# One cast queue in order of need for the loads of a fused attention and MLP kernel, with the first batch's scores ahead of v

## Chip, cores and metric

One core of one Trainium2 chip. The metric is device time in microseconds (us), the median over runs of one execution each. Fast runs of one kernel mostly lie within one per cent of each other (the kernel before: 267.07 to 270.18 us over all its runs); each comparison below is with runs of the kernel before on the same chip, interleaved with it. A run is called slow when it is over 1.5% above the fastest of its kernel; slow runs are left out of ratios. In the views PE is TensorE, DVE VectorE, ACT ScalarE, POOL GpSimd and SP SyncE; the granted clock is the share of TensorE's full clock that the throttle allowed. A casting DMA turns float32 into bfloat16 on the way.

## The reference

```python
# q, k, v: (8, 8, 576, 64); phi: (8, 8, 576, 32); x has 512 columns
a = softmax(phi, over the sequence)             # 32 memory slots per head
k_m, v_m = a^T k, a^T v                         # pooled: 32 x 64 per head
attn = softmax(q k_m^T / 8) v_m                 # (8, 8, 576, 64)
x = attn with the heads side by side            # (8, 576, 512)
xn = layer norm of x, times g_ln
out = x + relu(xn @ w_ch1) @ w_ch2              # 512 -> 2048 -> 512
```

## The kernel before

The kernel works one batch at a time. For each batch: exp of phi, pooling of k and v (`a_kv`), transposes of the pooled tiles (`a_tr`), q transposed (`a_qT`), scores (`a_sc`), denominators (`a_den`), a first-layer weight folded with the pooled v (`a_w1b`; the tile is `w1b`), the exp of the scores divided by the denominators (the tile `Eh`), then the first layer (`mm1`) and, during the next batch's attention, the second (`mm2`). All 16 DMA engines load the weights W1 and W2 and the first two batches' inputs meanwhile.

```python
def load_kv(b):
    t = inp.tile([P, 4, 2, NS * D], BF16, name="kv_bf")
    if b == 2:
        # "the hold": batch 2's loads wait for the last quarter of W2
        nc.gpsimd.tensor_copy(out=t[0:1, 0, 0, 0:1], in_=w2b[0:1, 15, 0:1])
    for slot, src in ((0, k), (1, v)):
        nc.gpsimd.dma_start(out=t[:, :, slot, :], in_=rows(src, b))   # casts to bf16
    return t
...
for n in range(NCH):                       # W1, cast, on the GpSimd queue
    nc.gpsimd.dma_start(out=w1r[:, :, fs], in_=w1_v[:, :, fs])
kv1 = load_kv(1)
q1 = load_q(1)
nc.gpsimd.dma_start(out=w2b[:, 12:16, :], in_=w2_v[:, 12:16, :])
def w2_load(n, queue):                     # W2's quarters 0 to 2: float32, staged
    ...
    queue.dma_start(out=st, in_=w2_v[:, 4 * n:4 * (n + 1), :])
def w2_cast(n):                            # and cast on GpSimd
    nc.gpsimd.tensor_copy(out=w2b[:, 4 * n:4 * (n + 1), :], in_=w2_st[n])
...
def a_qT(b, i):
    if b > 0:                              # batches 1 to 7: by DMA, from SyncE's queue
        nc.sync.dma_start_transpose(out=s["qT"]..., in_=s["q"]...)
        return
    ...                                    # batch 0: on TensorE, with copies out of PSUM
```

The order in which the opening is written, which engines follow as it stands:

```python
a_kv(0); a_tr(0); a_sc(0); w1_mean(0); ... a_w1b(0, 0); a_den(0); ...     # batch 0
mm1(0, ...)
for n in range(3): w2_cast(n)
...
mm2_quarter(0); a_kv(1); a_qT(1, 0); mm2_quarter(1); ...
a_tr(1); a_w1b(1, 0); mm2(0, 0, 8, 12); a_w1b(1, 1); mm2(0, 1, 8, 12); a_sc(1); ...
mm2(0, 2, 8, 12); a_w1b(1, 2); mm2(0, 3, 8, 12); a_den(1); mm2(0, 0, 12, 16); a_w1b(1, 3)
mm2(0, 1, 12, 16); ... x_tiles(0, [4, 5]); ...
load(2, phi2)
```

The softmax here doesn't subtract the row's maximum and nothing guards it: scores larger than these inputs give would overflow.

## Time and profile before

| | before |
|---|---|
| median | 268.2 us (267.88 to 268.77, 3 runs) |
| span of the profiled run | 268.4 us (device time 270.18 us), mean granted clock 0.984 |
| first layer of batch 0 ends | 35.7 us |
| DMA transpose of batch 1's q | 44.95 to 53.46 us |
| scores of batch 1 begin | 53.6 us |
| first layer of batch 1 ends | 72.7 us |
| from there to the end | 195.7 us |

The profiled run was a long one: its device time is 2 us over the median, since a span is some 1.8 us shorter than the device time of the same run.

The last row is the steady part, in which PE is at its limit. So the row to watch is the one above it: what the opening wins or loses shows in the end of batch 1's first layer.

### The profile page before, as it was taken

How to read it: one execution, taken by the hardware profiler on the slowest of the kernel's cores; microseconds unless marked ns; L12 is line 12 of the kernel's file. 1: busy time of each engine (PE TensorE's matmuls, PEld its weight loads, DVE VectorE, ACT ScalarE, POOL GpSimd, SP SyncE). 2: the span in 40 equal slices, each digit the busy share in tenths (PEclk: the TensorE clock that was granted, in tenths of full speed). 3: DMA queues.
4: the chain of work that ended last, by engine and by line, in shares of the span. 5: the costliest groups of instructions: out<-in, count | busy, mean ns of one | idle time of the engine just before them, and what ended most of it. 6: DMA issues, size and time to landing. Idle time of an engine off the chain costs nothing.

```text
span 268.4 us, 5722 instructions
## 1 busy us (share of the span) xinstructions
PE 249.3 (93%) x2437; PEld 137.2 (51%) x2437; DVE 153.3 (57%) x302; ACT 128.0 (48%) x218; POOL 30.2 (11%) x47
## 2 busy tenths in 40 slices
PE   6887897698999999999999999999999999999992
PEld 4653554134754476447643575447543664466440
DVE  2227652439447853777385943795386646783431
ACT  3166661055725456347636284448435472555210
POOL 8310022820030001200120003000000000000000
PEclk9999999689999999999999999999999999999998
DMA  6999999999999356984798194956621471120233
GB/s 195 227 206 219 295 283 295 157 199 218 258 160 223 82 144 125 161 183 85 181 169 175 41 238 70 221 123 150 80 65 44 86 190 42 43 61 17 46 74 78
DMA packets 45058, 39.63 MB, mean 148 GB/s; under 512 B 19940, under 2 KB 38376, under 8 KB 45032
## 3 DMA queue, kind: packets, MB, share of 16 engines
q0 software_dynamic: 14784, 16.19, 36.7%
q1 hardware_dynamic: 29720, 22.49, 35.0%
q10 hardware_dynamic: 528, 0.59, 0.7%
q8 instruction: 19, 0.31, 0.4%
q14 instruction: 7, 0.06, 0.1%
HBM read 41.42 MB, written 9.44 MB: 189 GB/s over the span
## 4 chain that ended last, share of the span: by engine, by line
PE 71%; DMA 19%; ACT 4%; DVE 3%; issue 1%; DVEq 0%; POOLq 0%
PE ch_ps L397 40%; PE h_ps L339 21%; DMA q_bf<-in_q_dram 12%; DMA kv_bf<-in_k_dram 4%; DMA qT<-q_bf 3%; PE o_ps L367 3%; PE w1b_ps L318 2%; PE kv_ps L208 2%; DVE Eh L303 2%; ACT rden L300 1%; PE sc_ps L281 1%; ACT x_sb L371 1%; DVE bst L375 1%; PE den_ps L298 1%; PE kv_ps L215 1%
## 5 line engine op out<-in xcount | busy, mean ns | idle before, releaser
L397 PE MATMUL ch_ps<-w2b,rT 128*128 128x512 bf16 x576 | 136.4, 384 | 3.0 <-POOL w2b L148 3.0
L397 PEld LDWEIGHTS <-rT 128*128 128x128 bf16 x576 | 54.4, 98 | 66.4 <-issue 11.8
L339 PE MATMUL h_ps<-Eh,w1b 128*128 128x288 bf16 x512 | 66.9, 285 | 3.5 <-ACT rT L345 1.7
L345 ACT ACTIVATE rT<-h_ps 128x576 bf16<-128x576 f32 x88 | 52.5, 649 | 31.2 <-PE h_ps L339 31.0
L339 PEld LDWEIGHTS <-w1b 128*128 128x128 bf16 x512 | 49.5, 97 | 20.8 <-issue 5.1
L322 DVE SCALAR_TENSOR_TENSOR w1b<-m_sb,rsum,w1b_ps 128x512 bf16<-128x512 f32 x64 | 43.6, 738 | 8.3 <-PE w1b_ps L318 6.2
L347 DVE TENSOR_SCALAR rT<-h_ps 128x576 bf16<-128x576 f32 x40 | 30.2, 756 | 27.3 <-PE h_ps L339 27.3
L405 DVE SCALAR_TENSOR_TENSOR x_sb<-ch_ps,rstd,x_sb 128x512 f32<-128x512 f32 x36 | 26.6, 742 | 16.1 <-PE ch_ps L397 16.1
L371 ACT ACTIVATE x_sb<-o_ps 128x1024 f32<-128x1024 f32 (+1 forms) x20 | 18.7, 939 | 35.3 <-PE o_ps L367 35.3
L375 DVE BATCH_NORM_STATS2 bst<-x_sb 128x6 f32<-128x512 f32 x36 | 24.4, 677 | 8.3 <-ACT x_sb L371 8.3
L286 ACT ACTIVATE E_sb<-sc_ps,rs 128x640 bf16<-128x640 f32 x16 | 11.8, 791 | 20.2 <-PE sc_ps L281 20.2
L303 DVE SCALAR_TENSOR_TENSOR Eh<-E_sb,rs,rden 128x576 bf16<-128x576 bf16 x16 | 12.4, 814 | 14.7 <-ACT rden L302 14.7
L83 POOL DMA_DIRECT2D kv_bf<-in_k_dram x8 | 6.2, 770 | 101.3 <-PE kv_ps L215 100.2
L383 ACT ACTIVATE rstd<-mv,eps_sb 128x2 f32<-128x2 f32 (+1 forms) x20 | 5.9, 294 | 16.3 <-DVE mv L376 16.3
L187 PE MATMUL w_ps<-vmask,blk 128*128 128x256 bf16 x72 | 11.1, 319 | 2.4 <-DVE vmask L130 2.4
L367 PE MATMUL o_ps<-vb,Eh 128*128 128x256 bf16 (+1 forms) x80 | 12.0, 276 | 1.0 <-DVE Eh L303 1.0
L318 PE MATMUL w1b_ps<-w1r,kvT 64*32 64x512 bf16 x256 | 11.6, 390 | 1.1 <-DVE kvT L239 0.6
L300 ACT ACTIVATE rden<-den_ps 128x576 f32<-128x576 f32 x16 | 9.6, 644 | 4.2 <-PE den_ps L298 4.1
L226 DVE CAST v<-kv_ps 128x128 bf16<-128x128 f32 x8 | 2.3, 290 | 15.7 <-ACT k L224 15.7
L196 ACT ACTIVATE e_sb<-phi_st 128x1152 bf16<-128x1152 f32 x8 | 9.2, 1151 | 2.7 <-DMA phi_st<-in_phi_dram 2.7
L187 PEld LDWEIGHTS <-blk 128*128 128x128 bf16 x72 | 7.9, 113 | 4.3 <-DVE blk L126 1.5
L302 ACT ACTIVATE rden<-rden 128x576 f32<-128x576 f32 x16 | 10.0, 682 | 0.0
(58 smaller groups left out, 115.4 us busy)
## 6 DMA issues: line engine op xcount, KB each, us to landing
out_dram<-x_sb SPq DMA_DIRECT2D x72, 128.0 KB, 2.4
kv_bf<-in_k_dram POOLq DMA_DIRECT2D x8, 576.0 KB, 6.4
kv_bf<-in_v_dram POOLq DMA_DIRECT2D x8, 576.0 KB, 9.7
phi_st<-in_phi_dram SPq DMA_DIRECT2D x7, 576.0 KB, 4.6
q_bf<-in_q_dram POOLq DMA_DIRECT2D x7, 576.0 KB, 11.1
w_st<-in_moe_w_ch_dram SPq DMA_DIRECT2D x3, 1024.0 KB, 16.2
w1r<-in_moe_w_ch_dram POOLq DMA_DIRECT2D x4, 512.0 KB, 17.2
q_st<-in_q_dram SPq DMA_DIRECT2D x1, 1152.0 KB, 10.8
```

The source lines that it names most:

```text
L187: nc.tensor.matmul(w_ps[:, 0:256], blk, vmask.rearrange("p j d -> p (j d)"), start=True, stop=True)
L303: nc.vector.scalar_tensor_tensor(out=Eh[:, g, :], in0=s["E"][:, g, 0:S], scalar=s["rs"][:, g:g + 1], in1=rd[:, g].rearrange("p a x -> p (a ...
L318: nc.tensor.matmul(ps[32 * j:32 * (j + 1), g, :], s["kvT"][r:r + 64, 2, 32 * j:32 * (j + 1)], w1r[r:r + 64, j, fs], start=True, stop=True, ...
L322: nc.vector.scalar_tensor_tensor(out=s["w1b"][:, g, fs], in0=m_sb[:, fs], scalar=s["rsum"][:, g:g + 1], in1=ps[:, g, :], op0=ALU.mult, op1 ...
L339: nc.tensor.matmul(h_ps[:, half, 0:HS], s["w1b"][:, g, P * j:P * (j + 1)], s["Eh"][:, g, HS * half:HS * (half + 1)], start=(g == 0), stop= ...
L345: nc.scalar.activation(out=dst, in_=h_ps[:, :, 0:HS], func=AF.Relu)
L347: nc.vector.tensor_scalar(out=dst, in0=h_ps[:, :, 0:HS], scalar1=0.0, scalar2=None, op0=ALU.max)
L367: nc.tensor.matmul(ov[:, :, g, :], s["Eh"][:, g, a:z], s["vb"][:, g].rearrange("p j d -> p (j d)"), start=True, stop=True)
L371: nc.scalar.activation(out=x[:, 0:n], in_=o_ps[:, 0:n], func=AF.Copy)
L375: nc.vector.bn_stats(out=stt, in_=x[:, i, :])
L397: nc.tensor.matmul(ch_ps, rT[:, j, P * t:P * (t + 1)], w2b[:, j, :], start=(j == 0), stop=(j == JC - 1))
L405: nc.vector.scalar_tensor_tensor(out=x, in0=ch_ps, scalar=rstd, in1=x, op0=ALU.mult, op1=ALU.add)
```

## The change

The intent: drop the float32 staging of W2 and its casts on GpSimd; put everything except phi of most batches on one casting queue, in the order in which it is needed (batch 1's phi, q, k and v between W2's quarters); load q of batch 0 first; and in batch 0 pool and score k before v arrives. With it the order of batch 1's attention among the second-layer groups changes.

```diff
 def load_kv(b):
-    if b == 2:
-        nc.gpsimd.tensor_copy(out=t[0:1, 0, 0, 0:1], in_=w2b[0:1, 15, 0:1])
...
-kv1 = load_kv(1)
-q1 = load_q(1)
-nc.gpsimd.dma_start(out=w2b[:, 12:16, :], in_=w2_v[:, 12:16, :])
-w2_load(0, nc.sync)          # staged, cast later on GpSimd by w2_cast
-w2_load(1, nc.sync)
-w2_load(2, nc.sync)
+w2_load(0)                   # now a casting DMA on the GpSimd queue
+phi1 = load_phi(1, nc.gpsimd)
+q1 = load_q(1)
+w2_load(1)
+kv1 = load_kv(1)
+w2_load(2)
+w2_load(3)
...
-a_kv(0)
-a_tr(0)
-a_sc(0)
+a_k(0)
+a_tr(0, v_part=False)
+a_sc(0)
+a_v(0)
+a_den(0)
+a_tr(0, k_part=False)
...
-for n in range(3):
-    w2_cast(n)
 a_exp(1)
+a_qT(1, 0)                   # the DMA transpose is now issued before the second layer
...
 mm2_quarter(0)
-a_kv(1)
-a_qT(1, 0)
 mm2_quarter(1)
+a_kv(1)
...                           # w1b(1, 1..3) later, between the last second-layer groups;
                              # x tiles 4 and 5 moved from here into batch 1's loop
```

Cut: `phi_st` gets two buffers instead of one, the warm-up matmuls at the start become fewer, and half of the copies of batch 0's transposed q go to DVE.

## The prediction

> **What bounds the kernel now.** I read the page first, then the chain that ended last, then clock and timeline of the first 75 us. From 67 us on the kernel is a stream of matmuls; what can change lies before.
>
> ```profile
> PE   6887897698999999999999999999999999999992
> PEclk9999999689999999999999999999999999999998
> DMA  6999999999999356984798194956621471120233
> ```
>
> Each digit is 6.7 us. PE is full except in the first eight slices, and DMA is full in just these. The only clock loss, the 6 and the 8, lies at 47 to 60 us. The chain says what the start waits for:
>
> ```profile
> 1.23 11.54 DMA kv_bf<-in_k_dram
> ...
> 13.06 31.87 DMA q_bf<-in_q_dram
> ...
> 44.95 8.51 DMA qT<-q_bf
> ...
> 53.60 0.74 PE sc_ps L281 x13
> 54.33 1.40 PE ch_ps L397 x4
> ```
>
> Columns: start, length. Batch 1's q stood in the queue behind W1 and k and v until 44.95, and its transpose behind that, so batch 1's scores began only at 53.60. The second thing on the path is W2:
>
> ```profile
> 47.01 1.89 POOL L148 CAST w2b<-w_st 128x2048 bf16<-128x2048 f32 x1 [4.80 <-DMA w_st<-in_moe_w_ch_dram]
> 48.95 1.86 PE L397 MATMUL ch_ps<-w2b,rT 128*128 128x512 bf16 x4 [1.92 <-POOL w2b L148]
> ```
>
> A staged part landed at 47.0, its cast on POOL took 1.89 us, and PE stood for it. The clock, by microsecond (the column after POOL's count is PEclk):
>
> ```profile
> 47.00:48.00 1.00, 0.03 (x8) 0.06 (x1) 0.89 (x2) 0.00 (x0) 0.99 (x1) 1.00 2.29 175
> 48.00:49.00 1.00, 0.04 (x1) 0.04 (x1) 0.51 (x1) 0.00 (x0) 0.90 (x1) 0.67 0.76 90
> 49.00:50.00 1.00, 1.00 (x3) 0.35 (x3) 0.00 (x0) 0.00 (x0) 0.18 (x1) 0.50 0.28 42
> ...
> 55.00:56.00 1.00, 1.00 (x11) 0.25 (x10) 0.00 (x0) 0.61 (x1) 0.19 (x1) 0.92 1.19 200
> ```
>
> The stall put PE at half clock from 48.34 (0.67 in that microsecond) to 55.16: 6.8 us, some 3 us lost. After that the end of the stage belongs to DVE:
>
> ```profile
> 59.32 1.55 DVE L303 SCALAR_TENSOR_TENSOR Eh<-E_sb,rs,rden 128x576 bf16<-128x576 bf16 x2 [1.77 <-ACT rden L302]
> 60.78 0.75 DVE L405 SCALAR_TENSOR_TENSOR x_sb<-ch_ps,rstd,x_sb 128x512 f32<-128x512 f32 x1
> 61.44 1.40 DVE L322 SCALAR_TENSOR_TENSOR w1b<-m_sb,rsum,w1b_ps 128x512 bf16<-128x512 f32 x2
> ...
> 67.08 5.63 PE L339 MATMUL h_ps<-Eh,w1b 128*128 128x288 bf16 x44 [0.74 <-ACT rT L345]
> ```
>
> The first-layer matmuls of batch 1 run freely only from 67.08 and end at 72.71. At the steady 7.95 us for all 64 (chain, later batches), they behave as if begun at 64.76: 3.9 us after Eh ends at 60.87. I call this the flow start; from there before and after are alike.
>
> **What the Trainium skill says.** (1) "DMA: Bandwidth & Descriptors", "Issuing engines are not separate DMA queues": DMAs of all issuers run on the same 16 engines, so another queue adds no bandwidth. The trace agrees: the cast queue alone wrote 0.41 MB in 2 us (18 to 20 us), so read 0.82 MB of float32: 410 GB/s. Cast queue and staged loads together, 32 to 36 us, read 0.41x2+0.73=1.55 MB in 4 us: 388 GB/s. (2) Same page, "Where 436 GB/s comes from", gives a 435 GB/s ceiling; 410 is near it. So one queue changes the order, hardly the sum. (3) "TensorE: Matmul & The Clock Gate", Part 1: the clock is halved after an idle window of 3413 ns and the window is free-running. 48.34 to 55.16 is two such windows; the one that led to the drop (44.9 to 48.3) was still about half busy, so in this trace half idle is enough. (4) Same page, "Architectural detail": DVE and ACT are strictly first in, first out; so the order in the program counts below.
>
> **The change part by part.** *Bytes.* The same 16.6 MB of float32 come before the last of W2. *First batch.* q goes first, as a cast (0.8 and 1.15 us of copies go); k is scored before v lands. By the queue's behaviour at 50 us (first landing 6.4 us after issue, the next ones 3.3 and 2.9 apart) I get q 7.5, k 10.8, v 13.7 us. Scores end about 14, against 18.6 before. But DVE now has Eh ahead of v's kvT, rsum, m_sb and w1b: from the score exp to Eh's end takes 5.1 us as before (18.49 to 23.6), so Eh ends at 18.8; then 0.28+0.28+0.69+1.40 us gives w1b at 21.4. Before, the flow began with Eh at 23.6. So the first-layer matmuls start 2.2 us sooner and end, after the same 11.9 us, at 33.3 (before 35.5).
>
> *Queue.* At 2.53 us per W part (0.52 MB written at 207), 2.85 per k, q, v and 1.5 for phi: W1 16.2 to 23.8; W2 part 0 26.3; phi 27.8; q 30.7; W2 part 1 33.2; k 36.1; v 38.9; W2 part 2 41.4; part 3 44.0. Into this falls q's DMA transpose, now from 31 us, in full traffic. Its engine share in the steady state (the queue's 101, 115 and 82% of three stretches of 2 us, less the phi and output bytes in them) is about 4.5 us; phi of batch 2 adds 1.5. So v lands at about 43.5, W2 part 2 at X = 47.2, part 3 at 49.9. Part 3 before landed at 49.6: the byte sum is not beaten.
>
> *PE.* From 33.3: outputs 1.0, two W2 quarters 3.6 each, so at 41.5 it waits for v till 43.5, pools 1.2, waits again till X. No POOL cast (1.89) stands in the path any more, but the data themselves come late.
>
> *Tail.* From X at full clock: quarter-tile of mm2 0.87, transposes 0.28, 0.87, scores 0.45, exp, w1b wait, four more groups 1.7, denominators at X+5.1, Ln and Exp, Eh ends X+8.8. In the built program's order DVE then has: out 0.75, w1b 1.40, out 0.75, w1b 1.40, out 0.75, w1b 1.40, out 0.75 = 7.2 us. Two of the three large PSUM buffers turn over while the second-layer tile holds the third, and the waits of the built program confirm it: the last w1b waits for DVE's second, the last mm2 group for tile 2's output, the third first-layer group for tile 3's. Two groups (1.0 us) run in the shadow, so the flow start is Eh + 6.2, against Eh + 3.9 before. x_tiles 4 and 5 move into the loop: +0.7.
>
> *Sum.* Eh at 47.2+8.8 = 56.0 instead of 60.87: -4.9. Tail +2.3, moved tiles +0.7: 268.2-4.9+3.0 = **266.3** at full clock. PE is nearly empty twice: 41.5 to 47.2, and X+8.8 to X+14.7, where only 1.2 us of work lies. Each is longer than a window, and each halving may cost up to 2.5 us (5 us at half). Before, one such loss was in Eh's 60.87, too. Since the first may be hidden in part by waits on exp, I add 1.5 in all: **267.8**.
>
> **Rivals.** *Data early.* Transpose and phi take less of the engines, X is 43.5, no first stall. Eh then ends 52.3 and the sum is 268.2-8.6+3.0 = 262.6, with the second halving 264 to 265. For it: no casts and a purer queue. Against: part 3 stood at 49.6 before with the same bytes. *Clock twice.* Both halvings in full: 266.3+5 = 271.3, and with X at 48.5 some 272.5. For it: in the trace 50% idle sufficed. *Hidden anyway.* All gains of the start end in the DMA queue, the time stays at 268; that is close to my sum. *Steady state disturbed*, by the second phi buffer or later loads: against it, kv of batch 2 is in the queue by 31 us and lands about 56, long before its use near 70.
>
> **Range and chances.** The low end is the data-early case, the high end the clock-twice one. Faster than 262.84 needs X near 43 and nearly no second clock loss: 0.12. Slower than 273.6 needs late data and both halvings: 0.09. Within 2%: 0.79. Time 267.8 us, range 263.0 to 272.5.
>
> **What would show it.** Right: first-layer matmuls of batch 0 from about 21.5; POOL without casts; PE waiting on v and W2 part 2 between 41 and 48; scores of batch 1 near 49, not 53.6; Eh of batch 1 near 56 to 58; DVE unbroken for 7 us after it with PE waiting on w1b and x_sb; PEclk dips near 45 and 58; batch 1's first-layer matmuls ending at 70 to 73. The prediction is wrong if W2 part 2 lands by 43, if DVE is done with w1b before Eh, or if the clock holds through both gaps.

## More of the kernel before

The lines of the profile that carry the table stand in the prediction. One reading that it doesn't have, the DMA view of the microsecond from 50 to 51 (columns: packets, MB, share of the 16 engines), becomes important later:

```profile
q1 hardware_dynamic: 1061, 0.27, 120.8%
```

This is the transpose of batch 1's q, alone on the engines: 1061 packets of some 256 bytes in one microsecond.

## The result, and the profile after

The changed kernel took 280.26, 281.44 and 281.02 us in its fast runs, against 268.49 us (267.88 to 269.05, 4 runs) before. A ratio in this document is the mean time of one kernel's fast runs over that of the other's of the same rounds, so not quite the ratio of the medians quoted. It is 1.0463 here (95% interval 1.0421 to 1.0505): slower, where the prediction had 267.8 us and at most 272.5. A fourth run took 499.27 us at a clock of 1.0. It counted as slow, nothing like it came back in any later run of any kernel, and its cause stays open; it is used nowhere.

| | before | after | predicted |
|---|---|---|---|
| first layer of batch 0 ends | 35.7 | 38.0 | 33.3 |
| DMA transpose of batch 1's q | 8.51 us | 23.56 us | some 4.5 us of the engines' time, issued at 31 |
| scores of batch 1 begin | 53.6 | 56.4 | about 49 |
| Eh of batch 1 ends | 60.9 | 65.8 | 56 to 58 |
| first layer of batch 1 ends | 72.7 | 81.0 | 70 to 73 |
| from there to the end | 195.7 | 197.5 | 195.7 + 0.7 |

The page of the profile after, engines and clock by slices of 7 us:

```profile
PE   6657999086899899999999999999999999999992
PEclk9988999859799999999999999999999999999999
DMA  7999999999838916597469549894711391111133
```

PE's 0 in the eighth slice (49 to 56 us) is new; the half clock follows it. W2 and v, on which the prediction let PE wait, were in time: PE ran the two quarters of the second layer at 38.7 to 45.7 us and v's pooling right after, at 45.7. What stopped it was q. The chain that ended last (start, length, what):

```profile
13.14 19.51 DMA q_bf<-in_q_dram
...
32.74 23.56 DMA qT<-q_bf
56.30 0.14 issue
56.44 0.51 PE sc_ps L299 x7
```

The transpose was issued at 32.74, twelve us sooner than before, and landed at 56.30, three us later than before. The DMA view of 44 to 46 us, in the middle of it (packets, MB, share of 16 engines), says why:

```profile
q0 software_dynamic: 308, 0.31, 91.3%
q1 hardware_dynamic: 308, 0.08, 29.7%
```

The numbers of packets are equal: q0 is the queue of the casts, q1 that of the transpose. A packet of q0 carried about 1 KB (0.31 MB / 308), one of q1 256 bytes. In turns, one against one, the transpose gets 154 packets per us where it had 1061 alone. A transpose of a 128 x 2560 bfloat16 tile is 2560 packets of 256 bytes; at 154 per us that is an estimate of 16.6 us, to which the first four us without any packet of it, and stretches with some 100 per us, add up to the 23.56.

The Trainium skill states the rule, in "DMA: Bandwidth & Descriptors", section "Queues, rings and completion order": each engine "round-robins between the queue rows it has work for, at *packet* granularity". The trace agrees in the turns, with 308 beside 308. The page's packet is several descriptors ("≈9-17 descriptors typical"); what the profile counts here is records of 256 bytes and of 1 KB, and whether each of them is a packet in the page's sense is not shown. The prediction used another section of the same page and drew the weaker conclusion from it, that the sum of bandwidth stays.

Why the cast queue was full that long shows on the timeline of the issuing engines (start, length, engine; SPq is the queue of SyncE):

```profile
28.99 0.74 POOL L79 DMA_DIRECT2D kv_bf<-in_k_dram  x1 [2.10 <-DMA w2b<-in_moe_w_ch_dram]
...
32.74 11.72 SPq L276 DMA_TRANSPOSE qT<-q_bf  x1
```

POOL issued batch 2's k at 28.99 us, its v and q by 32.94. They stood in the cast queue behind W2, whose last part landed at 49.3 us; k landed at 53.8 and v at 58.0, so the queue never ran dry until the transpose was through. Before, the same load went out at 50.23.

The wait costs more than its length. By stretches of 2 us (columns: length, then busy time with count of PE, PEld, DVE, ACT, POOL, then granted PE clock, DMA share, GB/s):

```profile
50.00:52.00 2.00, 0.00 (x0) 0.00 (x0) 0.00 (x0) 0.00 (x0) 0.00 (x0) 1.00 1.39 144
52.00:54.00 2.00, 0.00 (x0) 0.00 (x0) 0.00 (x0) 0.00 (x0) 0.00 (x0) 0.77 1.15 191
54.00:56.00 2.00, 0.00 (x0) 0.00 (x0) 0.00 (x0) 0.00 (x0) 0.00 (x0) 0.50 1.24 195
...
62.00:64.00 2.00, 2.00 (x13) 0.88 (x11) 0.00 (x0) 1.51 (x3) 0.00 (x0) 0.67 1.22 208
```

PE did nothing from 48.8 to 56.4, the clock fell to half at about 53 and came back at about 63, so some 6 us of work after the wait ran at half speed.

Then the tail, in the words of the prediction, on DVE and PE (PE's line last):

```profile
65.75 0.74 DVE L423 SCALAR_TENSOR_TENSOR x_sb<-ch_ps,rstd,x_sb 128x512 f32<-128x512 f32 x1
66.41 1.40 DVE L340 SCALAR_TENSOR_TENSOR w1b<-m_sb,rsum,w1b_ps 128x512 bf16<-128x512 f32 x2
...
70.49 1.86 PE L415 MATMUL ch_ps<-w2b,rT 128*128 128x512 bf16 x4 [2.23 <-DVE x_sb L423]
```

And the opening, where PE stood still inside one group of v's pooling:

```profile
15.79 0.52 PE L187 MATMUL kv_ps<-kv_bf,e_sb 64*32 64x64 bf16 x45 [0.18 <-DMA kv_bf<-in_v_dram]
18.98 0.40 PE L187 MATMUL kv_ps<-kv_bf,e_sb 64*32 64x64 bf16 x27 [2.67 <-issue]
```

"issue" means that PE waited for nothing that the profile shows: 2.67 us after the 45th of 72 equal matmuls.

### The profile page after: what moved, and what is told of

The parts are those of the page before. It is cut to its first block, busy times and chain, and to the rows that moved or that the text cites. A ratio compares the mean times of both kernels' runs of the same rounds, so it can differ in the third digit from the quotient of the medians.

```text
span 278.5 us, 5782 instructions
## 1 busy us (share of the span) xinstructions
PE 245.2 (88%) x2455; PEld 136.5 (49%) x2486; DVE 153.7 (55%) x303; ACT 125.5 (45%) x216; POOL 27.3 (10%) x46
## 4 chain that ended last, share of the span: by engine, by line
PE 65%; DMA 19%; DVE 7%; ACT 4%; issue 2%; POOL 0%; DVEq 0%; SPq 0%; POOLq 0%
PE ch_ps L415 36%; PE h_ps L357 20%; DMA qT<-q_bf 8%; DMA q_bf<-in_q_dram 7%; DMA kv_bf<-in_k_dram 4%; PE o_ps L385 3%; DVE Eh L321 2%; PE w1b_ps L336 2%; PE kv_ps L187 2%; DVE bst L393 2%; ACT rden L318 2%; DVE w1b L340 1%; DVE x_sb L423 1%; ACT x_sb L389 1%; PE sc_ps L299 1%
## 5 line engine op out<-in xcount | busy, mean ns | idle before, releaser
L415 PE MATMUL ch_ps<-w2b,rT 128*128 128x512 bf16 x547 | 131.2, 385 | 5.0 <-DVE x_sb L423 2.2
L423 DVE SCALAR_TENSOR_TENSOR x_sb<-ch_ps,rstd,x_sb 128x512 f32<-128x512 f32 x36 | 26.8, 743 | 16.3 <-PE ch_ps L415 15.7
L304 ACT ACTIVATE E_sb<-sc_ps,rs 128x640 bf16<-128x640 f32 x16 | 11.8, 790 | 18.3 <-PE sc_ps L299 18.3
L299 PE MATMUL sc_ps<-qT,kvT 64*32 64x320 bf16 x128 | 4.2, 321 | 8.2 <-DMA qT<-q_bf 7.6
L187 PE MATMUL kv_ps<-kv_bf,e_sb 64*32 64x128 bf16 (+1 forms) x648 | 7.3, 217 | 3.2 <-issue 2.7
```

What stands on the lines that cost most here:

```text
L415: nc.tensor.matmul(ch_ps, rT[:, j, P * t:P * (t + 1)], w2b[:, j, :], start=(j == 0), stop=(j == JC - 1))
L423: nc.vector.scalar_tensor_tensor(out=x, in0=ch_ps, scalar=rstd, in1=x, op0=ALU.mult, op1=ALU.add)
```

## Experiments

**The theory**: the loss is the transpose sharing the engines packet for packet with a cast queue that batch 2's loads keep full, and the half clock after the wait. **Rivals**: the order of the tail on DVE, or the new opening of batch 0, is what costs; or the new queue itself is bad. For the stop in v's pooling there are two more: that it is tied to a place in PE's program (instructions fetched late), or to the pooling itself or the time. A is the theory, B its opposite, and C the rival on the opening; D and E are, for the stop, the place in the program and the other reading. The experiments came in three groups (1 to 4, 5 to 8, 9 to 12); each group ran on one chip, interleaved with the kernel before.

### 1. The hold put back

```diff
 def load_kv(b):
     t = inp.tile(..., name="kv_bf")
+    if b == 2:
+        nc.gpsimd.tensor_copy(out=t[0:1, 0, 0, 0:1], in_=w2b[0:1, 15, 0:1])
```

> The changed kernel, but k and v of batch 2 are held back until the last part of W2 has landed, as the kernel before did. Theory A (the transpose of batch 1's q is starved: it gets one small packet for every packet of the cast queue, about 150 a microsecond each, for as long as that queue has work): the queue runs dry at about 50 us, the transpose then finishes at about 51 to 52 instead of 56.3, and the time falls by 4 to 6 us, to 275 to 277. Theory B (the transpose is slow by itself in this place, or its wait is covered by something else such as DVE's chain): no change, 280 to 282.

Measured: 272.1 us median (271.45 to 273.64), ratio to before 1.0140 (1.0086 to 1.0194), against 1.0463 without the line. One instruction of 0.18 us brings back some 9 us of the 12.5, more than the 4 to 6 expected. The DMA view of 46 to 48 us:

```profile
q1 hardware_dynamic: 632, 0.16, 85.1%
q0 software_dynamic: 155, 0.15, 43.5%
```

As the casts ran out at about 46.5 us, the transpose took the engines alone, and landed after 17.72 us instead of 23.56; scores began at 51.2, with a wait of 1.50 us instead of 7.65, and the clock held at 1.00 there. The end of batch 1's first layer moved from 81.0 to 74.8. This shows the main cause. The transpose is still twice as long as before the change, since W2's own casts share with it for 10 us.

### 2. Batch 1's q transposed on TensorE instead

```diff
 def a_qT(b, i):
-    if b > 0:
+    if b > 1:
...
     a_qT(1, 0)
+    a_qT(1, 1)
```

> The changed kernel, but batch 1's q is transposed on TensorE as batch 0's is; no DMA transpose before batch 2. Theory A: the 7.65 us wait of the scores and the half clock after it (52.9 to 62.7) go; 1.3 us of transposes come; scores of batch 1 at 49 to 50, first-layer matmuls of batch 1 end at 72 to 74 instead of 81.0, time 271 to 274. Theory B (DVE's chain at the stage's end and the lost clock are the cost, whatever the scores wait for): over 277.

Measured: 274.1 us (272.31 to 275.19), ratio 1.0199 (1.0129 to 1.0269). No hold here; the cast queue is as full as in the changed kernel, and nothing transposes beside it. Scores began at 51.4 without a wait for q, as with the hold. So it is the meeting of the two that costs, not the one queue: taking away either side gives most of it back. What is left of the loss shows in the same tail as in the changed kernel (waits of 2.2 us on x_sb and 1.7 on w1b, half clock from about 61.5 to 68 us).

### 3. Batch 0 in the old order

```diff
-    a_k(0)
-    warm(3)
-    a_tr(0, v_part=False)
+    a_kv(0, False)
+    warm(2)
+    a_tr(0)
     warm(2)
     a_sc(0)
-    a_v(0)
-    a_den(0)
-    a_tr(0, k_part=False)
     w1_mean(0); m_copy(0); a_w1b(0, 0)
+    a_den(0)
```

> The changed kernel, but batch 0 is pooled and scored in the order of the kernel before (k and v together, then transposes, scores, first W1 part, then denominators). Theory A says the end of the stage is set by the transpose at 56.3 in any case, so the time stays within 1 us of 281. Theory C (the slow start, with PE's stop of 2.67 us inside v's pooling and the half clock after it, is handed down to the end): the start's first-layer matmuls begin about 2 us sooner and the time falls by 2 us or more. In any case the stop inside the pooling should be gone if it comes from the number of PE instructions issued in the burst.

Measured: 281.1 us (280.31 to 281.85), ratio 1.0467, the same as with the split. Batch 0's first layer ended 0.8 us sooner (37.2), the stop in the pooling was gone, and PE then waited 8.40 us for the transpose instead of 7.65. As long as the transpose ends the stage, the opening of batch 0 is hidden behind it.

### 4. The kernel before without its hold

```diff
 def load_kv(b):                 # of the kernel before
-    if b == 2:
-        nc.gpsimd.tensor_copy(out=t[0:1, 0, 0, 0:1], in_=w2b[0:1, 15, 0:1])
```

> The kernel before without its hold on batch 2's k and v. Theory A: batch 2's loads now share the engines with batch 1's transpose from about 45 us, it lands at 57 to 59 instead of 53.5 and the time rises by 3 to 5 us, to 271 to 273. Theory B: no change, 268 to 269.

Measured: 272.0 us (268.67 to 272.76; one run called slow), ratio 1.0089 (1.0006 to 1.0171). So the hold alone, taken from the kernel before, costs about 1% (0.1 to 1.7%), not 4.6%. The transpose landed at 54.5 us, not at the 57 to 59 expected. POOL's timeline says why:

```profile
46.41 1.90 POOL L145 CAST w2b<-w_st 128x2048 bf16<-128x2048 f32 x1 [3.90 <-DMA w_st<-in_moe_w_ch_dram]
48.25 0.75 POOL L80 DMA_DIRECT2D kv_bf<-in_k_dram  x1
```

Batch 2's loads come after W2's casts in POOL's program, and POOL takes its program in order, so it reached them at 48.25: only 2 us sooner than with the hold (50.23). Its waits for the staged W2 were a second hold that nobody had written as one. The transpose took 10.7 us instead of 8.5. The change removed both holds at once, and the loads went out at 28.99.

### 5. TensorE transposes and the old tail

The edit of experiment 2, and the order of batch 1's attention among the second-layer groups as before:

```diff
-    mm2(0, 0, 8, 12)
     a_tr(1)
+    a_w1b(1, 0)
+    mm2(0, 0, 8, 12)
+    a_w1b(1, 1)
     mm2(0, 1, 8, 12)
     a_sc(1)
...
-    mm2(0, 3, 12, 16)
+    mm2(0, 2, 12, 16, finish=False)
+    mm2(0, 3, 12, 16, finish=False)
+    x_tiles(0, [4, 5])           # back from batch 1's loop
+    mm2_out(0, 2)
+    mm2_out(0, 3)
```

> Batch 1's q transposed on TensorE (as the run that did that alone, 274.1 us) and, besides, the end of the opening stage in the order of the kernel before: three of batch 1's four first-weight products ahead of the denominators, outputs of tiles 2 and 3 after all second-layer groups, tiles 4 and 5 in the opening. Theory A with the DVE chain as second cost: in the run without this order, 7.2 us of DVE work lay behind the last Eh (56 to 57 us), PE stood 1.7 and 2.2 us and ran at half clock for 7 us, so batch 1's first-layer matmuls ended at 74.5; here they should end at 68 to 70 and the time be 267 to 270. If that chain was covered anyway, 273 to 275.

Measured: 271.5 us (270.96 to 272.02), ratio 1.0135 (1.0105 to 1.0164), 0.6% better than experiment 2, which ran in another group. It lies between the two expectations (267 to 270, or 273 to 275), and 68 to 70 us for the end of batch 1's first layer was missed. That end came hardly sooner than in experiment 2 (74.0 against 74.5), but in this run the opening had been slower: the clock was half from about 14.5 to 28 us and batch 0's first layer ended at 40.0, against 38.9. From the end of batch 0's first layer to that of batch 1's it took 33.9 us, against 35.6. The steady part took 195.9 us from there, against 197.7: moving x tiles 4 and 5 into the loop cost some 1.7 us there. Of that, 0.74 us are their six matmuls, which ran in the opening before; the rest is not explained. Over the profiled runs of both kernels and of experiments 1 to 5, all fast, the steady part is 197.1 to 197.7 where these tiles sit in the loop and 195.6 to 195.9 where they don't.

### 6 and 7. The kernel before with the new queue only

The kernel before, its opening and its tail, with W2 unstaged and the new order on the cast queue. In 6 there is no hold and q of batch 1 goes over TensorE; in 7 the hold is kept and the DMA transposes.

```diff
-kv1 = load_kv(1)
-q1 = load_q(1)
...                              # staging and w2_cast removed
+w2_load(0); phi1 = load_phi(1, nc.gpsimd); q1 = load_q(1)
+w2_load(1); kv1 = load_kv(1); w2_load(2); w2_load(3)
+# 6: no hold, "if b > 1" in a_qT, a_qT(1, 0) and a_qT(1, 1) after a_exp(1)
+# 7: hold, "if b > 0" in a_qT
```

> The kernel before with its own start and matmul order, but with the change's queue (W2 unstaged, phi, q, k and v of batch 1 between W2's parts, all on one queue) and batch 1's q transposed on TensorE; no hold of batch 2's loads. If the queue order is good by itself and only the DMA transpose and the new matmul order spoil it, this is faster than before: no wait on POOL casts (3.0 us), none on the transpose, no half clock at 48 to 55: 261 to 264. If the queue itself loses (data of W2 or v too late), 267 or more.

> As the run before in this call (new queue, start and matmul order of the kernel before), but with batch 1's q transposed by DMA and the hold on batch 2's k and v kept. Theory A: the transpose is issued at 31 to 33 us, shares packet for packet with the queue until that is empty, lands at 49 to 52, and the scores, due at about 47 in this order, wait 3 to 5 us: 265 to 268, that is 3 to 5 us above the TensorE version. Theory B: the same time as the TensorE version or less, since PE has 20 transposes fewer.

Measured: 6 took 269.1 us (268.27 to 270.76), ratio 1.0053 (1.0009 to 1.0096); 7 took 269.3 (268.5 to 269.34), ratio 1.0046 (1.0017 to 1.0074). The gains hoped for (261 to 264, and 265 to 268) were missed; both times fall under the other branch of their expectation. There is no difference between the two.

In 7 the transpose took 17.3 us beside the casts, as in experiment 1 (309 and 312 packets in 44 to 46 us), but was issued at 33.4 and landed at 50.7, before PE had come to the scores in either kernel (52.4 and 52.8 us, with no wait for q in either). A starved transpose that lands in time holds up no scores. It was not free, though: batch 1's v landed 20.9 us after its issue, where it took 19.8 in 6, and PE, which had ended batch 0's first layer 1.7 us sooner than in 6 (36.6 against 38.3), waited for it and then ran at half clock from 43.9 to 46.9 us:

```profile
42.75 0.80 PE L197 MATMUL kv_ps<-kv_bf,e_sb 64*32 64x128 bf16 x72 [1.87 <-DMA kv_bf<-in_v_dram]
```

At the start of 6, at 10 to 12 us, the turns show with the cast queue as the victim:

```profile
q0 software_dynamic: 224, 0.24, 70.0%
q1 hardware_dynamic: 222, 0.27, 45.0%
```

Here q1 carries phi of batch 2. With the second `phi_st` buffer it needs to wait for nobody, so it is loaded at 9 to 16 us, packet for packet beside batch 0's v: PE waited 2.35 us for v, pooled only at 17.1 us (15.6 before), and batch 0's first layer ended at 38.3 (35.7 before). That this is what 6 lost is not shown by the profiles: 7 loads this phi just as early (225 and 222 packets in the same 2 us) and pooled v at 15.3 us. Experiment 12 takes the early load away.

### 8. The kernel before, TensorE transposing batch 1's q

```diff
-    if b > 0:
+    if b > 1:
...
     a_kv(1)
-    a_qT(1, 0)
     mm2_quarter(1)
+    a_qT(1, 0)
+    a_qT(1, 1)
```

> The kernel before with nothing changed but batch 1's q transposed on TensorE (after the second quarter of W2, when q has landed, at about 45 us). Theory A: the transpose no longer holds the scores till 53.6, and the last part of W2 gets its engines alone; but the POOL casts still stop PE and the clock: 265 to 268.

Measured: 267.7 us (266.87 to 270.21), ratio 1.0009 (0.9957 to 1.0061). It lies in the expected 265 to 268, but so does the kernel before. In the profiled run, which was the fastest, scores began at 50.2 instead of 53.6, the clock loss near 50 us was gone, and batch 1's first layer ended at 69.1 instead of 72.7. These 3.6 us are not what the transposing DMA costs. The spread of the four runs is 3.3 us, and the timing shows no gain; the profile of the kernel before is of a run 2 us over its median, in which PE waited only 0.40 us for q; and batch 0's first layer, up to which the two programs are alike, had already ended 1.1 us sooner (34.6 against 35.7). A cost of the transpose in the kernel before is not shown.

### 9. The stop in v's pooling

```diff
-    warm(24)
+    warm(12)
```

> The changed kernel with 12 instead of 24 warming matmuls at the very start, so that every later PE instruction stands 24 places earlier in PE's program (a matmul is two instructions). In all four runs of the split start so far PE stopped for 2 to 2.7 us after exactly 45 of the 72 matmuls that pool v, with nothing to wait for. Theory D (PE has run ahead of the loading of its own program, whose 16 KB piece stands in the DMA engines behind the queue): the stop stays at the same place in the program, that is after 57 of the 72. Theory E (something in the pooling itself, a PSUM or data wait that the profile does not show): it stays after 45.

Twelve fewer warm-up matmuls ahead of everything, on the changed kernel, one look only (279.3 us, state unknown, and not used as a time):

```profile
16.95 0.68 PE L187 MATMUL kv_ps<-kv_bf,e_sb 64*32 64x64 bf16 x57
20.53 0.25 PE L187 MATMUL kv_ps<-kv_bf,e_sb 64*32 64x64 bf16 x15 [2.90 <-issue]
```

The stop moved from after the 45th matmul to after the 57th: by exactly the 12 that were taken away. It is tied to a place in PE's program, not to v, the PSUM tile or the time (it began 1.3 us later besides). In the changed kernel a packet of 16 KB of the queue marked as instructions crosses the DMA engines at 16 to 17 us, while the stop begins at about 16.3. In the other five kernels with this order of batch 0 such a packet crosses within 1 us of the beginning of the stop, too (at 16 to 17 us in 1 and 10, 17 to 18 in 2 and 5, 18 to 19 in 9). That PE waits there for its next instructions, behind a full cast queue, fits all this, though no run shows the fetch itself as the releaser. The Trainium skill, "Runtime: NRT & Kernel Launch", section "Instruction fetch mechanics", says that instructions are refilled in 16 KiB blocks and the cost of a boundary is "mostly hidden". The size agrees with the packet. If the stop is such a boundary, its cost was not hidden: it was 2.67 us here and 1.99 to 2.90 in the other five. The kernel before has its packet at 17 to 18 us and no stop.

### 10 and 11. The changed kernel, repaired part by part

10 is the changed kernel with the hold (experiment 1) and the old tail (of experiment 5), with the DMA transposing. 11 is 10 with batch 0 in the old order (experiment 3).

> The changed kernel with the hold on batch 2's k and v and with the end of the opening stage in the order of the kernel before; DMA transpose kept. With the hold alone it took 272.1 us, and DVE's chain behind Eh (PE idle 2.2 and 1.7 us, then half clock from 62 to 69 us) was the next cost. Theory A plus the DVE chain: 2 to 4 us less, 268 to 270. If the chain was covered: 272.

> As the run before in this call, but batch 0 is pooled and scored in the order of the kernel before (k and v together). With the transpose in the way this made no difference (281.1 against 281.2). If the split start costs by itself (PE's stop, Eh ahead of w1b on DVE), now that nothing hides it 1 to 2 us come off; if scoring k early gains anything, 1 us or more comes on.

Measured: 10 took 274.20, 273.98, 274.95 and 268.17 us; the three are over 1.5% above the fourth and so called slow, and there is no ratio. 11 took 267.51, 267.55 and 269.91 us in fast runs (a fourth, slow, 271.62), ratio 0.9987 (0.9943 to 1.0031). With hold, tail and batch 0 restored, what remains is chiefly the new queue (with q of batch 0 cast first and the second phi buffer), and it is level with the kernel before: neither a gain nor a loss is shown. The one fast run of 10 lies within the fast runs of 11, so a cost of the split start is not shown either.

The profiled run of 10 is a slow one, so it explains no difference, but it shows what the spread looks like inside: batch 1's first layer ended at 69.7 us, 3 us sooner than before, and then PE waited again for a transpose, that of batch 2's q, which took 18.5 us where it takes 5.5 in the kernel before:

```profile
84.15 0.73 PE L301 MATMUL sc_ps<-qT,kvT 64*32 64x320 bf16 x16 [5.05 <-DMA qT<-q_bf]
```

At 72 to 74 us its packets stand one to one with those of the casts (279 and 282). From 77 to 82 us few packets of either queue move, though from 79 us on the engines are marked busy; why is open, as is whether this is what the other two slow runs had.

### 12. The best version

Experiment 6 with one `phi_st` buffer instead of two, so that phi of batch 2 waits for batch 1's exp and keeps off the start:

```diff
-    t = inp.tile([P, 4, NS * M], FP32, name="phi_st")
+    t = inp.tile([P, 4, NS * M], FP32, name="phi_st", bufs=1)
```

> The new queue with the start and matmul order of the kernel before and batch 1's q transposed on TensorE, 269.1 us, but with one phi buffer as before instead of two. In that run phi of batch 2 was loaded at 9 to 16 us, because no transpose stood before it in its queue any more, and took a packet for each packet of batch 0's k and v, which landed at 17.1 instead of about 15. With one buffer phi of batch 2 waits for batch 1's exp at 36 us or later: v at 15 to 15.6, no half clock at 18 to 22, 265.5 to 267.5. This is the version meant to beat both kernels; if it is at 269 the early phi load was harmless.

Measured with five rounds: 267.0 us (265.96 to 268.45, 6 runs) against 268.64 (11 runs), ratio 0.9939 (0.9909 to 0.9969), while 6 had 1.0053 (1.0009 to 1.0096). Each is against the kernel before in its own group, and the two intervals do not meet: the second buffer cost about 1%. By which path is not settled: v was pooled at 16.3 us, not at the 15 to 15.6 expected, against 17.1 in 6 and 15.3 in 7, which has the second buffer as well. The clock by slices:

```profile
PEclk9999999999999999999999999999999999999999
```

There is no loss of clock left in the opening. Batch 1's first layer ended at 69.7 us (72.7 in the long profiled run before; the timings differ by 1.6 us) and the steady part took 195.8 as before. This beats both kernels; by 0.6%, which is within the 2% called the same.

## Why the prediction was wrong

- **The step that failed** is in the part on the queue: "Into this falls q's DMA transpose, now from 31 us, in full traffic. Its engine share ... is about 4.5 us". The prediction took the transpose as so much work to be inserted among the casts. In truth it got turns, and turns of a quarter of the size: 23.56 us from issue to landing. The prediction's list has a landing for v and for each part of W2, but none for the transposed q. So X, on which the sum rested, was not the last wait of the stage; q was. With the transpose put right, experiments 1 and 2 return 7 to 9 of the 12.5 us.
- **The other landings came out**, in part by luck: v at 42.7 (43.5 predicted), W2's part 2 at 46.0 (X = 47.2) and part 3 at 49.3 (49.9). The queue was some 2 us late (q of batch 1 landed at 32.7, not 30.7), and beside the transpose it slowed less than supposed, to three quarters: 308 packets in 2 us, 410 without a transpose in experiment 2. PE met no wait at 41 to 47 us because, after the late opening, it came to v only at 45.7 and to part 2 at 46.7.
- **The rival it dismissed** held the clue: "kv of batch 2 is in the queue by 31 us and lands about 56, long before its use near 70". It asked if these loads come in time, not whom they hold up until then. The hold was part of the diff, and so were POOL's casts, the second hold (experiment 4); the prediction gave neither a cost of its own.
- **The start** was wrong in sign: batch 0's first layer ended 2.2 us later instead of 2.2 sooner. q landed at 10.1, k at 12.9 and v at 15.8 us, where 7.5, 10.8 and 13.7 had been set; then came the stop of 2.67 us, which no view of the kernel before could show. In the changed kernel all this was hidden (experiment 3); whether it costs in the repaired one is not shown (10 gave one fast run, 268.17 us, and 11 took 267.51 to 269.91).
- **Eh** ended at 65.8 instead of 56.0: against the kernel before that is 5.0 later, of which 2.2 come from the start and the rest from q and the half clock.
- **The tail was right in its mechanism**: DVE worked without a gap for 5.9 us after Eh (7 predicted, with the last output, which waited 0.64 us for PE), PE waited on w1b and then on x_sb, and the clock halved again at 70 us. From Eh's end to the end of the first layer it took 15.2 us against 11.8 before, +3.3 unrounded; the prediction had +2.3 at full clock, and part of its 1.5 for halving.
- **The moved tiles** were set at 0.7 us and cost some 1.7 (experiment 5).
- **The clock**: 1.5 us were set aside for both halvings. The work from 56.4 to some 63.3 us ran at half clock, which alone is about 3.1 us lost, and the second halving came on top.
- **Readings to put right**: the DMA row isn't full "in just these" eight slices but to the thirteenth, at 87 us; what fills it after W2 are the later batches' loads, first the ones that the hold had kept back. The profile used was of a run of 270.18 us, while the sum starts from 268.2. And the 435 GB/s of point (2) is, in that section, the ceiling of the ports into SBUF, the on-chip memory, where this queue wrote 207; the 410 are what it read from HBM. What it concludes there then rests on point (1) alone.

The sum by the rows of the table: Eh +5.0 instead of -4.9, tail +3.3 instead of +2.3, steady part +1.8 instead of +0.7, together +10.1 between the two profiled runs (278.5 against 268.4). The timings differ by 12.5, since the profiled run of the kernel before was a long one and that of the changed kernel its shortest.

## What to carry to other kernels

When two DMA queues are loaded at once, count packets, not bytes: here they took turns (308 packets beside 308 in 2 us), so the queue with the smaller packets got the smaller share (0.08 MB beside 0.31), and a transpose that took 5.5 us in the steady part took 23.6. When removing a staging copy, a buffer limit or a touch that looks useless, ask what it held back: here one copy of one element and the waits of an in-order issuing engine kept batch 2's loads off the engines, and the second phi buffer let another load in at the start. Issuing early helps only what must be early; a load that is not needed for 50 us is best held until the critical ones have landed.

## What the Trainium skill lacked or had wrong

- "DMA: Bandwidth & Descriptors" has the rule of turns by packet, but not what follows for queues of unequal packets (308 packets each in 2 us, 0.31 MB against 0.08 MB), nor a warning for the DMA transpose: one of 2560 packets took 5.5 us in the steady part, 8.5 in the opening before, and 23.6 beside a full cast queue.
- "Runtime: NRT & Kernel Launch", "Instruction fetch mechanics", calls the cost of a block boundary mostly hidden. Here PE stood 1.99 to 2.90 us at a fixed place of its program while the cast queue was full; if that is a block boundary, which is inferred (experiment 9), it was not hidden.
- "TensorE: Matmul & The Clock Gate", Part 1, speaks of an idle window before the clock halves. In the kernel before, the 3.4 us ahead of the drop (44.9 to 48.34 us) were about half busy: PE worked 1.55 us of them.
